# A 1 MB DRAM-to-DRAM copy on the weight queue, at the end of each step of a recurrent attention kernel

## The chip, the core and the metric

The kernel runs on one core of a Trainium2 chip; the other cores do nothing. The metric is the device time of one execution in microseconds (us), as a median over repeated executions.

## What is computed

The output mixes two branches row by row: `g * a + (1 - g) * b`, with `g = sigmoid(sum(x * gate_w))`. Branch `b` is a gated feed-forward block. Branch `a` is attention over segments of 32 rows with a memory of 8 rows, and the memory that one segment leaves is an input of the next, so the 64 segments have to be worked one after the other.

```python
def _A_ref(x, mem0, Wq, Wk, Wv, Wo, seg_len):     # x: 1 x 2048 x 1024, 32 heads of 128
    mem = mem0                                     # 8 rows
    for s in range(n_seg):                         # 64 segments of 32 rows
        h = jnp.concatenate([mem, x[:, 32*s:32*s+32]], axis=1)          # 40 rows
        q, k, v = (jnp.einsum('btd,dhe->bhte', h, W) for W in (Wq, Wk, Wv))
        p = _softmax(jnp.where(mask, q @ k.T * scale, -1e9))
        o = jnp.einsum('bhte,hed->btd', p @ v, Wo)
        mem = o[:, :M]                             # rows 0..7 feed the next segment
        outs.append(o[:, M:])

def _B_ref(x, w_gate, w_up, w_down):               # 1024 -> 3584 -> 1024
    return _gelu(x @ w_gate) * (x @ w_up) @ w_down
```

All inputs are bf16. Each of the four attention weights Wq, Wk, Wv, Wo is 1024 x 32 x 128 (or its transpose), 8.4 MB[...].

## The kernel before

The program first transposes x and works a small part of the feed-forward block while the attention weights are loaded. Then come the 64 steps of the recurrence (`for s in range(NSEG)`), one per segment, each about 23.5 us long. Then the rest of the feed-forward block runs (`for fb in range(NFB)`), which also mixes and stores the output.

**One step.** The weights are cut into 64 pieces of 128 x 2048 bf16 (512 KB): 8 pieces for each of K, Q, V, O and each half `r` of the heads. A step is a walk over these 64 pieces in a fixed order (`walk`). It starts with K and Q of the first half, one piece of each in turn (`both(0)`), then V of the first half, then K and Q of the second half (`both(1)`), then O of the first half mixed with V of the second, and last O of the second half. `proj(p, s)` issues the matmuls of piece number `p`: lines L820 and L803 for K, Q and V, L831 for O. Between the pieces, the dictionary `at`, filled by calls `on(m, r, n, f)`, holds the other work: `f` is called ahead of piece `n` of the block `(m, r)`. The tails are L870 (an output projection of rows that were put off, tile `oR`), L850 (projections made ahead for a later group, tile `hR`) and L1042 (the new memory rows go into the next step's `hT`).

**The weight stream.** Most pieces stay resident in slots (`sl`). The pieces named in `PAIRS` (3 of K, none of Q, 5 of V, 4 of O) share a slot between the two halves of the heads, and have to be loaded again in each step: 3 + 5 + 3 pieces of 512 KB, and half a piece, 256 KB, into the tile `oh` (the other half of that O piece stays resident). `proj` ends with `spent(k)`, which issues the next load into the slot just read. All of these loads are issued from SyncE (SP), in the order of the program, on one hardware queue (L394 for `sl`, L387 for `oh`); SP waits on a semaphore of TensorE until the slot is free and then issues.

Every DMA belongs to a *lane*, a semaphore of its own; a DMA on a lane waits for the lane's previous DMA to have landed.

**The end of a step on SP.** After the load of `oh` follow the small loads for later steps: `qkr` (L551, 128 KB, for the next step), `hT` (L543, 64 KB, for the step after next) and two of `vB` (L557, 32 KB each, for the next step). SP then waits for the first K piece of the next step to have been used, and issues the three K loads. The stores run on other queues: `o_scr<-oRc` and `a_scr<-a_bf` (64 KB each a step) on ScalarE's queue, a few small ones on GpSimd's.

The place that the change touches:

```python
            if not last:
                on("o", 1, 0, lambda: load_qk(s + 1))
                if s + 2 < NSEG:
                    on("o", 1, 0, lambda: load_h(s + 2))
                on("o", 1, 0, lambda: load_v(s + 1))
            if s % 4 == 2 and G + 1 < NG:
                on("o", 1, 4, lambda: load_r(G + 1))
```

Of the kernel before, what the change touches and what calls it, by code (L numbers as in the profile page):

```python
# [5 lines left out]
BF16 = mybir.dt.bfloat16  # L6
# [24 lines left out]
class _Prog:  # L31
# [47 lines left out]
    def op(self, eng, fn, rd=(), wr=(), lane=None, after=()):  # L79
        o = _Op(eng, fn)  # L80
        if lane is not None:
            ln = self.lanes.get(lane)
            if ln is None:
                ln = self.lanes[lane] = [self.new_sem(f"{self.name}_{lane}"), 0, None]
            if ln[2] is not None:
                o.deps.append(ln[2])
            ln[1] += 16
            o.sem, o.val, o.inc, o.need = ln[0], ln[1], 16, True
            ln[2] = o
        for r in rd:  # L90
            self._touch(o, r, False, lane is not None)
        for r in wr:
            self._touch(o, r, True, lane is not None)
        o.deps.extend(after)
        if eng == "pool" and lane is None:
            if self.pool is not None:
                o.deps.append(self.pool)
            self.pool = o
        for d in o.deps:
            d.need = True  # L100
        o.idx = len(self.ops)
        self.ops.append(o)
        return o
# [92 lines left out]
def bass_gated_mix__memory_aug_recurrent_mem_tr__geglu_ffn__prompt_kernel(  # L196
# [16 lines left out]
    S, D = xf.shape  # L213
    _, H, Dh = A_Wq.shape
# [17 lines left out]
    with ExitStack() as es:  # L232
# [19 lines left out]
        NJP = 4  # L252
        NJR = NJ - NJP
        g_scr = nc.dram_tensor("g_scr", [NFB, 128, NJP * FB], BF16)

        PB = [es.enter_context(nc.psum_tensor(f"pb{i}", [128, 512], FP32)) for i in range(8)]
        PBV = [p[:, :].bitcast(BF16) for p in PB]
# [97 lines left out]
        op = P.op  # L355
# [185 lines left out]
        def load_h(s, eng="sp"):  # L541
            t = hTs[s % 2]
            op(eng, lambda e: e.dma_start(t[:, :, :].rearrange("p k c -> p (k c)"), xq_scr[s // 4, :, s % 4, :]),  # L543
               rd=[("D", "xq", s // 4)], wr=[t.r()], lane=f"h{eng}{s % 2}")

        def load_r(G):
            op("pool", lambda e: e.dma_start(hR[:, :, :].rearrange("p k c -> p (k c)"), xr_scr[G]), rd=[("D", "xr", G)],
               wr=[hR.r()], lane="hr")

        def load_qk(s):  # L550
            op("sp", lambda e: e.dma_start(qkr[:, :, :, :].rearrange("p u m c -> p u (m c)"),  # L551
                                           qk_scr[s // 4, :, :, s % 4, :].rearrange("u p c -> p u c")),
               rd=[("D", "qk", s // 4, u) for u in range(2)], wr=[qkr.r()], lane="qkr")

        def load_v(s, us=(0, 1), eng="sp"):
            for u in us:
                op(eng, lambda e, u=u: e.dma_start(vB[:, u, :], v_scr[s][:, u].rearrange("i h c -> h i c")),  # L557
                   rd=[("D", "v", s // 4, u)], wr=[vB.r(128 * u, 128 * u + 128)], lane=f"vb{eng}{u}")
# [4 lines left out]
           wr=[gwb.r()], lane="gw")  # L563
# [359 lines left out]
        for s in range(NSEG):  # L923
# [12 lines left out]
            def on(m, r, n, *fs):  # L936
                at.setdefault(spot["k" if m == "q" else m, r][n], []).extend(fs)
# [78 lines left out]
            if not last:  # L1016
                on("o", 1, 0, lambda: load_qk(s + 1))
                if s + 2 < NSEG:
                    on("o", 1, 0, lambda: load_h(s + 2))
                on("o", 1, 0, lambda: load_v(s + 1))  # L1020
            if s % 4 == 2 and G + 1 < NG:
                on("o", 1, 4, lambda: load_r(G + 1))

# [189 lines left out]
```

## Time and profile before

| | before |
|---|---|
| median of 13 executions | 2164.41 us (2155.23 to 2174.27) |
| the profiled execution, its own time | 2168.27 us |
| its span in the profile | 2166.3 us |
| TensorE busy | 1991.2 us, 92% of the span |
| bytes moved by DMA | 512.79 MB, of it 467.16 MB on SP's queue |
| steps of the recurrence | about 130 to 1630 us of the span |

The span is the part that the profile covers; 2.0 us of the execution lie outside it. A busy share says how long an engine had work in flight. The chain of waits follows the work that ended last back to what released each piece. In the list of DMA issues, the last number is the median time from issue to landing. In a table of windows, "DMA share" is the mean busy share of the core's 16 DMA engines in that stretch (slightly over 1 where a packet's time reaches out of it), and GB/s what they moved.

### The profile page before, as it was taken

To read this page: it belongs to the slowest core of one execution; us is meant where nothing else is said; L and a number is where in the kernel's file an instruction comes from. 1 tells how busy PE (TensorE), PEld (TensorE's weight loads), DVE (VectorE), ACT (ScalarE), POOL (GpSimd) and SP (SyncE) were. 2 spreads that over 40 slices of the span, in tenths; PEclk is the share of its full clock that TensorE was granted. 3 is DMA by queue.
4 is the path that set the end of the run, shared out by engine and by line. 5 is a ranking of instruction groups with operands and counts; after the bars stand their busy time and mean duration, and the time that the engine had idled before them with its cause. 6 is when DMAs were issued, how large, how long until landed. Compare 5 with 4: busy or idle time off the path is not lost.

```text
span 2166.3 us, 77621 instructions
## 1 busy us (share of the span) xinstructions
PE 1991.2 (92%) x38220; PEld 958.8 (44%) x32556; DVE 938.2 (43%) x2056; ACT 650.5 (30%) x1330; POOL 291.1 (13%) x589
## 2 busy tenths in 40 slices
PE   7888999989999998989899898989888999999999
PEld 4334454454444445445444444444344334243343
DVE  6433443443444443444344344434434436263462
ACT  4323333333333332333233233323222213032130
POOL 7211111111111111111111111111110000000000
PEclk9999999999999999999999999999999999999999
DMA  9988888887888887888888788878889200001000
GB/s 363 358 304 266 307 303 279 289 302 271 296 303 274 305 309 257 283 284 300 263 305 306 263 282 294 298 254 297 288 287 372 94 21 30 31 30 30 25 25 20
DMA packets 259310, 512.79 MB, mean 237 GB/s; under 512 B 56080, under 2 KB 109200, under 8 KB 258984
## 3 DMA queue, kind: packets, MB, share of 16 engines
q1 hardware_dynamic: 216256, 467.16, 62.1%
q10 hardware_dynamic: 34136, 20.19, 3.3%
q0 software_dynamic: 8592, 20.49, 2.6%
q8 instruction: 278, 4.55, 0.9%
q14 instruction: 48, 0.39, 0.1%
HBM read 474.17 MB, written 33.55 MB: 234 GB/s over the span
## 4 chain that ended last, share of the span: by engine, by line
PE 74%; DMA 19%; issue 4%; ACT 2%; DVE 1%; SPq 0%; POOL 0%; ACTq 0%; POOLq 0%; DVEq 0%
PE pb L820 17%; PE pb L480 17%; PE pb L803 13%; DMA oh<-in_A_Wo_dram 9%; PE pb L831 8%; DMA sl<-in_A_Wv_dram 5%; PE pb L850 4%; PE pb L708 4%; PE pb L1168 4%; PE pb L870 2%; PE pb L1146 1%; PE pb L772 1%; DMA xr_scr<-xr 1%; ACT a_bf L694 1%; ACT vA L694 1%
## 5 line engine op out<-in xcount | busy, mean ns | idle before, releaser
L820 PE MATMUL pb<-sl,hT 128*32 128x512 bf16 x8192 | 712.7, 383 | 26.5 <-DMA sl<-in_A_Wv_dram 16.2
L820 PEld LDWEIGHTS pb<-sl,hT 128*32 128x32 bf16 x8192 | 235.5, 97 | 403.1 <-issue 276.7
L803 PE MATMUL pb<-sl,hT 128*32 128x512 bf16 x4096 | 405.6, 383 | 0.0
L831 PE MATMUL pb<-sl,oT 128*32 128x256 bf16 x7680 | 292.8, 276 | 62.4 <-issue 42.2
L831 PEld LDWEIGHTS pb<-sl,oT 128*32 128x32 bf16 x7680 | 205.4, 97 | 114.0 <-issue 71.3
L850 PE MATMUL pb<-sl,hR 128*32 128x512 bf16 x3072 | 228.9, 387 | 19.9 <-issue 8.8
L694 ACT ACTIVATE tok<-pb 128x512 bf16<-128x512 f32 x192 | 114.9, 598 | 299.9 <-PE pb L820 273.8
L480 PE MATMUL pb<-xT,wg 128*128 128x512 bf16 x768 | 183.1, 382 | 4.0 <-DMA wg<-in_B_w_gate_dram 4.0
L480 PE MATMUL pb<-xT,wu 128*128 128x512 bf16 x768 | 181.5, 379 | 0.0
L468 ACT ACTIVATE s<-pb 128x512 f32<-128x512 f32 x112 | 66.9, 597 | 290.5 <-PE pb L480 290.5
L1168 PE MATMUL pb<-wd,GT 128*32 128x512 bf16 x1568 | 152.4, 379 | 0.0
L803 PE MATMUL pb<-wd,GT 128*32 128x512 bf16 x1568 | 152.4, 379 | 0.0
L797 POOL COPY oRc<-oT 128x128 bf16<-128x128 bf16 x128 | 96.5, 754 | 390.1 <-DVE oT L697 390.1
L697 DVE CAST oT<-pb 128x256 bf16<-128x256 f32 x256 | 96.8, 420 | 120.0 <-PE pb L784 120.0
L469 DVE SCALAR_TENSOR_TENSOR tp<-s,pb 128x512 f32<-128x512 f32 x112 | 76.7, 685 | 126.6 <-ACT s L468 126.2
L694 ACT ACTIVATE vA<-pb 128x512 bf16<-128x512 f32 x128 | 76.4, 597 | 171.7 <-PE pb L820 171.7
L850 PEld LDWEIGHTS pb<-sl,hR 128*32 128x32 bf16 x3072 | 86.7, 98 | 91.6 <-issue 34.2
L697 DVE CAST hT<-pb 128x32 bf16<-128x32 f32 x63 | 12.1, 191 | 254.9 <-PE pb L1042 254.9
L480 PEld LDWEIGHTS pb<-xT,wg 128*128 128x128 bf16 x768 | 75.0, 98 | 97.0 <-issue 8.2
L743 DVE TENSOR_REDUCE st<-pb 128x8 f32<-128x320 f32 x128 | 62.9, 492 | 125.3 <-PE pb L737 125.2
L480 PEld LDWEIGHTS pb<-xT,wu 128*128 128x128 bf16 x768 | 75.2, 98 | 90.9 <-issue 0.5
L697 DVE CAST stg<-pb 128x512 bf16<-128x512 f32 x64 | 44.3, 692 | 159.6 <-PE pb L803 159.6
(111 smaller groups left out, 2179.6 us busy)
## 6 DMA issues: line engine op xcount, KB each, us to landing
sl<-in_A_Wv_dram SPq DMA_DIRECT2D x331, 512.0 KB, 8.5
sl<-in_A_Wk_dram SPq DMA_DIRECT2D x205, 512.0 KB, 6.0
sl<-in_A_Wo_dram SPq DMA_DIRECT2D x204, 512.0 KB, 6.7
oh<-in_A_Wo_dram SPq DMA_DIRECT2D x65, 256.0 KB, 7.5
sl<-in_A_Wq_dram SPq DMA_DIRECT2D x16, 512.0 KB, 12.9
qkr<-qk_scr SPq DMA_DIRECT2D x63, 128.0 KB, 7.3
qk_scr<-fqk ACTq DMA_DIRECT2D x29, 256.0 KB, 5.9
wd<-in_B_w_down_dram SPq DMA_DIRECT2D x7, 1024.0 KB, 15.0
```

Source lines behind the costliest of these rows:

```text
L468: op("act", lambda e: e.activation(s1[:, :], hg, ACTF.Square, scale=SQ), rd=[BK(bg)], wr=[s1.r()])
L469: op("dve", lambda e: e.scalar_tensor_tensor(out=t[:, :], in0=s1[:, :], scalar=1.0, in1=hg, op0=ALU.add, op1=ALU.mult), rd=[BK(bg), s1.r() ...
L480: ins = e.matmul(PB[bk][:, 0:FB], lhsT=w[:, kc, cc:cc + 128], rhs=x[:, :, :, kc, :].rearrange("p t i c -> p (t i) c"), start=(kc == 0), st ...
L694: op("act", lambda e: e.activation(o, i, ACTF.Copy), rd=rd, wr=wr)
L697: op("dve", lambda e: e.tensor_copy(o, i), rd=rd, wr=wr)
L708: ins = e.transpose(to, t[:, j * 128:(j + 1) * 128], ident[:, :])
L797: op("pool", lambda e: e.tensor_copy(oRc[:, u, :, :].rearrange("p c (g j) -> p g j c", g=4), diag), rd=[oT.r()], wr=[oRc.r(128 * u, 128 * ...
L803: return e.add_instruction(mybir.InstMatmult(name=nc.get_next_instruction_name(), start_tensor_calc=start, stop_tensor_calc=stop, tile_siz ...
L820: ins = again(e, g, *at, one, end) if k[0] == "q" else e.matmul(*at, start=one, stop=end)
L831: ins = e.matmul(PB[XO][32 * g:32 * g + 32, 0:256], lhsT=oT[:, gp_, 2 * jj + hh, 0:32], rhs=w[:, c:c + 256], start=(r == 0 and one and hh ...
L850: ins = e.matmul(PB[b][32 * g:32 * g + 32, :], lhsT=h[:, k[2], :], rhs=w[:, g * 512:(g + 1) * 512], start=(n == 0), stop=(n == 7))
L1168: ins = again(e, q, *a, j == 0, j == NJ - 1) if hf else e.matmul(*a, start=(j == 0), stop=(j == NJ - 1))
```

## The change

A DRAM tensor `warm` of 1 MB is declared, and in each step but the last a copy of the first 128 rows of Wk (128 x 4096 bf16, 1 MB, contiguous) into it is issued from SP, ahead of piece 4 of the block `("o", 1)`. Nothing reads `warm`. Its lane, `warm`, makes each copy wait for the copy of the step before.

```diff
         g_scr = nc.dram_tensor("g_scr", [NFB, 128, NJP * FB], BF16)
+
+        warm = nc.dram_tensor("warm", [128, H * Dh], BF16)
...
                 if s + 2 < NSEG:
                     on("o", 1, 0, lambda: load_h(s + 2))
                 on("o", 1, 0, lambda: load_v(s + 1))
+                on("o", 1, 4, lambda: op("sp", lambda e: e.dma_start(warm[:, :], A_Wk[0:128].rearrange("d h e -> d (h e)")),
+                                         wr=[("D", "warm", 0)], lane="warm"))
             if s % 4 == 2 and G + 1 < NG:
                 on("o", 1, 4, lambda: load_r(G + 1))
```

## Prediction, made before the changed kernel was run

> **What bounds the kernel now.** I read the page's slices first, then the chain of waits, then one step in the timeline of SP and in tables of windows.
>
> ```profile
> PE   7888999989999998989899898989888999999999
> DMA  9988888887888887888888788878889200001000
> PE 74%; DMA 19%; issue 4%; ACT 2%; DVE 1%; SPq 0%; POOL 0%; ACTq 0%; POOLq 0%; DVEq 0%
> ```
>
> TensorE is nearly full everywhere, the DMA engines are eight tenths full for as long as the recurrence lasts, and the chain passes through both. Neither number says what a megabyte more costs, so I look at one step (start, duration, line, what is issued):
>
> ```profile
> 1025.32 0.47 SPq L387 DMA_DIRECT2D oh<-in_A_Wo_dram  x1
> 1025.83 0.43 SPq L551 DMA_DIRECT2D qkr<-qk_scr  x1
> 1026.73 0.34 SPq L543 DMA_DIRECT2D hT<-xq_scr  x1
> 1027.83 1.16 SPq L557 DMA_DIRECT2D vB<-v_scr  x2
> 1033.97 1.30 SPq L394 DMA_DIRECT2D sl<-in_A_Wk_dram  x3
> 1037.43 2.33 SPq L394 DMA_DIRECT2D sl<-in_A_Wv_dram  x5
> ```
>
> and at the chain of waits in the same place:
>
> ```profile
> 1025.32 5.37 DMA oh<-in_A_Wo_dram
> 1030.69 0.04 issue
> 1030.73 0.40 PE pb L831 x7
> 1031.13 1.12 issue
> ```
>
> The loop of a step is: the first K slot is freed, the stream of 11 pieces and `oh` (5.77 MB) runs, `oh` lands last, TensorE finishes the step in about 3.2 us (1030.73 to 1033.97), and the next K slot is freed. The stream's end gates TensorE, so what delays the stream delays the step. Only the hole between two streams is free DMA time. Its size, in windows from 3.4 us ahead of the first K issue to 0.85 us behind it (last two columns: DMA share, GB/s), in three consecutive steps:
>
> ```profile
> 1006.88:1011.13 4.25, 3.15 (x80) 1.83 (x72) 0.19 (x1) 0.96 (x3) 0.29 (x1) 1.00 0.30 73
> 1030.57:1034.82 4.25, 2.93 (x72) 1.49 (x64) 0.62 (x2) 0.58 (x2) 0.34 (x1) 1.00 0.27 69
> 1053.53:1057.78 4.25, 3.81 (x96) 1.46 (x72) 0.88 (x2) 1.18 (x3) 0.42 (x2) 1.00 0.26 61
> ```
>
> The next three such steps have shares 0.22, 0.31 and 0.37. The mean is 0.29, so the hole holds 0.71 x 4.25 = 3.0 us of every engine's time.
>
> How the stream starts matters too. After the hole it is slow, while TensorE works `both(0)`; it is fast in the V block and slower again in `both(1)`, with no hole in front of that:
>
> ```profile
> 1034.82:1036.82 2.00, 2.00 (x44) 0.47 (x20) 0.00 (x0) 0.00 (x0) 1.99 (x4) 1.00 0.93 203
> 1037.40:1039.80 2.40, 2.40 (x64) 1.26 (x56) 0.92 (x2) 0.98 (x3) 0.00 (x0) 1.00 0.99 379
> 1039.80:1043.30 3.50, 3.50 (x72) 0.95 (x36) 2.71 (x8) 0.99 (x3) 0.22 (x1) 1.00 0.99 322
> 1043.30:1046.70 3.40, 3.38 (x124) 2.43 (x115) 1.93 (x5) 2.17 (x5) 1.25 (x3) 1.00 1.02 410
> ```
>
> The first 2.0 us give 192, 203, 242, 197, 195 and 206 GB/s in the six steps, mean 206.
>
> [...] SP's list of instructions for the changed kernel gives the copy as 16 x 32768, so all 16 engines work, 64 KB each; no copy of this kind is in the trace. [...] the queue named "instruction" moved 4.55 MB in 278 packets, 16.4 KB each.
>
> **The change, part by part.** It removes and moves nothing.
>
> *Issue on SP.* 63 more issues, at about 0.43 us (1.30 us for three K loads). SP is free from 1028.99, behind `vB`, until 1033.97, and the copy goes there. Its wait is for the copy of a step ago, about 23 us before. Nothing is queued behind it but the K loads, which wait for TensorE anyway. Cost nothing; the cover is 5.0 us.
>
> *The hole.* Issued at about -4.5 us before the first K load, and with some 0.9 us from issue to first data (1033.97 to the restart in the window at 1034.82), [...].
>
> *How long the copy holds an engine.* No DRAM-to-DRAM transfer is in the trace. Lower bound: the rate of the loads, 410 GB/s, makes 1.05 MB / 410 = 2.6 us. [...]
>
> *The stream.* [...] the K loads start 2.0 us late. They miss the slow 2.0 us: 206 x 2.0 = 412 KB, less the 64 KB of `a_scr` on another queue, so about 347 KB. If the slow start belongs to TensorE's `both` block, as the second slow stretch without a hole suggests, these bytes are made up at the end of the stream at about 390 GB/s, which is 0.9 us. If it belongs to the stream's own start, it moves along, and the full 2.0 us are lost. I take 0.9.
>
> *What of it reaches TensorE.* In some steps the queue runs dry before the O loads and swallows a delay. In the page `oh` needs 7.5 us to land in the median, against 5.37 in the step above, whose queue was short. So most steps have a backlog in front of `oh`. I choose 0.9 as the share that passes: 0.9 x 0.9 = 0.8 us a step. What is late next is `oh`, and the V pieces before it (L820 waits for them already).
>
> *Instruction blocks.* TensorE's "issue" idle ahead of L831 is its own starvation, around the end of a step:
>
> ```profile
> PE pb L831 <- issue: 45.7, 43, 2.2
> ```
>
> A fetch that falls beside the copy may wait behind a copy packet. Bounds: nothing, if packets are short or the block early; 1.1 us a step (45.7 / 43), if one more such stall arises in every step. I choose 0.3.
>
> *Other queues.* `o_scr` and `a_scr` stores share engines with the copy and land some us later. `a_bf` shares its place with the softmax tile `tA`, written some 9 us after that store's issue; cost nothing, unless the store takes that long.
>
> *Sum.* 63 x (0.8 + 0.3) = 69 us on the profiled execution's 2168.3 us, so 2237 us. That execution stands 3.9 us above the median of 2164.4, so I predict 2233 us.
>
> **The rivals.**
> 1. *The slow start moves with the stream* (22%). 2.0 x 0.9 + 0.3 = 2.1 us a step, 132 us, about 2297 us. For it: every stream starts at about 206. Against: the stretch at 1039.80.
> 2. *The copy fits the hole* (20%). [...] Only the instruction term is left, 0 to 19 us: 2164 to 2183 us. For it: the lower bounds. [...]
> 3. *Faster* (8%). The 206 GB/s is the price of a queue that had run empty, at the place of the first two K loads. A copy that bridges the hole saves up to (390 - 206) x 2.0 / 390 = 0.94 us a step. It decides below 3.0 + 0.94 = 3.9 us for the copy; at 3.0 us it makes 0.94 x 0.9 x 63 = 53 us, so 2111 us. Against: TensorE's block explains the slow stretches without it.
> 4. *Much slower* (10%). The copy takes 7 us or more, or instruction blocks stand behind 64 KB packets in each step: over 2310 us. [...]
>
> That the copy isn't made, or goes elsewhere, is excluded by SP's list: 63 more entries, each between `vB` and the first K load.
>
> **How the numbers follow.** My own case has 40%, 2195 to 2265 us. Against no change, a measurement of this kernel can tell about 0.3%, or 6.5 us. Rival 2 falls mostly within that or a little above: 12% for the same, 8% slower. Slower then is 40 + 22 + 8 + 10 = 80%, faster 8%. The range runs from 2157, the foot of rival 2, to 2310 us, and leaves out rivals 3 and 4.
>
> **What would show it.** In the profile after: 63 copies of 1024 KB on SP with a time to landing of about 6 to 7 us; 66 MB more written; a DMA share near 1 where it was 0.29; the first K piece landing about 2 us later against its issue; steps of about 24.6 us instead of 23.5; more time of the chain on `oh` and V. I am wrong if the copy lands within 4 us of issue, if the stream after it starts at over 350 GB/s, or if the steps grow while the K loads don't land later (then it is the instruction blocks).

## The result, and the profile after

| | before | after |
|---|---|---|
| median | 2165.88 us (48 executions) | 2201.58 us (11 executions, 2193.05 to 2214.12) |
| ratio to before, 95% interval | | 1.0167 (1.0146 to 1.0187) |
| span of the profiled execution | 2166.3 us | 2199.8 us |
| moved on SP's queue | 467.16 MB | 533.23 MB |

The kernel is slower by 1.7%, some 36 us or 0.57 us for each of the 63 copies. I had predicted 2233 us and a range of 2157 to 2310: the direction and the range hold, and the size is half of what I forecast.

The page of the changed kernel, slices and chain of waits, with the line on the DRAM:

```profile
PE   7888889998988898898999988999888999999999
DMA  9989999999999988999999999999999300000000
HBM read 540.23 MB, written 99.61 MB: 291 GB/s over the span
PE 67%; DMA 25%; issue 4%; ACT 2%; DVE 1%; POOL 0%; SPq 0%; ACTq 0%; POOLq 0%; DVEq 0%
```

The DMA digits went from 8 to 9 over most of the recurrence, the writes grew by 66.06 MB (63 copies of 1.05 MB), and DMA's share of the chain from 19 to 25%. TensorE's line of the page, before and then after:

```profile
PE 1991.2 (92%) x38220; PEld 958.8 (44%) x32556; DVE 938.2 (43%) x2056; ACT 650.5 (30%) x1330; POOL 291.1 (13%) x589
```

```profile
PE 2000.9 (91%) x38220; PEld 954.4 (43%) x32556; DVE 940.2 (43%) x2056; ACT 650.5 (30%) x1330; POOL 291.0 (13%) x589
```

The same 38220 matmuls kept it busy 9.7 us longer, so only 23.8 of the span's 33.5 us are idle time.

The copy sits where SP's list put it (timeline of SP, one step of the changed kernel):

```profile
1058.30 1.93 SPq L389 DMA_DIRECT2D oh<-in_A_Wo_dram  x1
1062.52 1.18 SPq L559 DMA_DIRECT2D vB<-v_scr  x2
1063.74 0.60 SPq L1023 DMA_DIRECT2D warm<-in_A_Wk_dram  x1
1068.25 2.47 SPq L396 DMA_DIRECT2D sl<-in_A_Wk_dram  x3
1071.70 2.61 SPq L396 DMA_DIRECT2D sl<-in_A_Wv_dram  x5
```

and it goes into the hole. These are windows from 3.4 us ahead of the first K issue to 0.85 us behind it in three steps of the changed kernel; the last two columns are DMA share and GB/s, as before:

```profile
1064.85:1069.10 4.25, 3.34 (x80) 1.64 (x72) 0.62 (x2) 0.58 (x2) 0.34 (x1) 1.00 1.01 320
1087.76:1092.01 4.25, 3.61 (x88) 1.27 (x64) 0.88 (x2) 1.18 (x3) 0.29 (x1) 1.00 0.94 299
1111.44:1115.69 4.25, 3.58 (x84) 1.23 (x64) 0.88 (x2) 1.18 (x3) 0.29 (x1) 1.00 0.92 291
```

The share there was 0.22 to 0.37; now it reads 0.92 to 1.01. That is too much: a table of windows counts a packet whole where it starts, and the copy's packets are long. With each packet's time counted only where it lies (worked out from the packets in the traces, from the third step to the last), the share of the hole goes from 0.26 to 0.83, and in the second profiles of the two kernels from 0.27 to 0.78.

The stream behind it starts worse. First three steps of before, then three of after, 5 us from 0.85 us behind the first K issue:

```profile
1011.13:1016.13 5.00, 5.00 (x112) 2.02 (x84) 1.12 (x2) 1.40 (x3) 0.00 (x0) 1.00 0.95 298
1034.82:1039.82 5.00, 5.00 (x112) 2.02 (x84) 1.12 (x2) 1.40 (x3) 2.35 (x5) 1.00 0.96 298
1057.78:1062.78 5.00, 5.00 (x88) 2.19 (x68) 1.54 (x3) 1.73 (x3) 0.00 (x0) 1.00 0.89 215
```

```profile
1069.10:1074.10 5.00, 5.00 (x112) 2.02 (x84) 1.12 (x2) 1.41 (x3) 2.35 (x5) 1.00 0.89 270
1092.01:1097.01 5.00, 5.00 (x88) 2.19 (x68) 1.54 (x3) 1.73 (x3) 0.00 (x0) 1.00 0.78 232
1115.69:1120.69 5.00, 5.00 (x88) 2.19 (x68) 1.54 (x3) 1.73 (x3) 0.00 (x0) 1.00 0.88 261
```

Single steps vary, but over six steps the means are 292 GB/s before and 252 after (over all from the third, 289 and 252). In 5 us that is 0.20 MB less, and at the 390 GB/s of the later stream 0.5 us a step. The lower share of these windows is not idle time: counted where it lies, the packets' share is 0.93 before and 0.94 after. The engines are still at work on the copy.

The packets show how far. The copy is 1008 packets of 65536 bytes, 16 for each copy. One takes 3.07 us in the median (2.4 to 4.7), and in 62 of the 63 copies all 16 are in flight together, for 1.4 us in the median. The copy is issued 4.0 us ahead of the first K issue in the mean; its first packet starts 2.4 us ahead of it, the last one 0.8 us ahead, and the last one ends 2.1 us behind it (2.3, 0.7 and 2.3 in the second profile). What spreads the starts over 1.6 us isn't shown: the trace doesn't name a packet's engine. By the shares above, 0.7 us of the hole stay empty on the average engine (0.9 in the second profile), and 0.5 us of the copy (0.6) lie behind the hole, where the K loads should run. The first K piece lands 5.8 us after its issue in the median (5.7 in the second profile) instead of 4.6.

The list of DMA issues (last number: median us to landing; K was 6.0 and `o_scr` 3.2 before):

```profile
sl<-in_A_Wk_dram SPq DMA_DIRECT2D x205, 512.0 KB, 7.0
warm<-in_A_Wk_dram SPq DMA_DIRECT2D x63, 6.5
o_scr<-oRc ACTq DMA_DIRECT2D x64, 64.0 KB, 6.2
```

Waits that are new (engine, what waited, for what: us in total, times, longest). The first line is of before, the other three of after:

```profile
PE pb L820 <- DMA sl<-in_A_Wk_dram: 0.7, 1, 0.7
```

```profile
PE pb L822 <- DMA sl<-in_A_Wk_dram: 8.0, 16, 1.0
PE pb L774 <- DVE tA L755: 6.3, 3, 2.8
DVE tA L755 <- DMA a_scr<-a_bf: 11.5, 4, 4.6
```

K pieces now come too late in 16 places at that line (1 and 3 in the two profiles of before), and in four steps the store of `a_bf` landed so late that the softmax tile sharing its place had to wait, and in three of them TensorE with it.

### The profile page after: what moved, and what is told of

It reads as the page before. It is cut to its first block, busy times and chain, and to the rows that moved or that the text cites. A ratio compares the mean times of both kernels' runs of the same rounds, so it can differ in the third digit from the quotient of the medians.

```text
span 2199.8 us, 77684 instructions
## 1 busy us (share of the span) xinstructions
PE 2000.9 (91%) x38220; PEld 954.4 (43%) x32556; DVE 940.2 (43%) x2056; ACT 650.5 (30%) x1330; POOL 291.0 (13%) x589
## 3 DMA queue, kind: packets, MB, share of 16 engines
q1 hardware_dynamic: 218272, 533.23, 69.5%
## 4 chain that ended last, share of the span: by engine, by line
PE 67%; DMA 25%; issue 4%; ACT 2%; DVE 1%; POOL 0%; SPq 0%; ACTq 0%; POOLq 0%; DVEq 0%
PE pb L482 16%; PE pb L822 14%; DMA oh<-in_A_Wo_dram 12%; PE pb L805 11%; PE pb L833 7%; DMA sl<-in_A_Wk_dram 5%; PE pb L1172 4%; PE pb L852 4%; PE pb L710 4%; DMA sl<-in_A_Wv_dram 3%; DMA a_scr<-a_bf 2%; PE pb L872 2%; PE pb L1150 1%; DMA xr_scr<-xr 1%; PE pb L774 1%
## 5 line engine op out<-in xcount | busy, mean ns | idle before, releaser
L822 PE MATMUL pb<-sl,hT 128*32 128x512 bf16 x8192 | 717.8, 384 | 49.8 <-issue 22.0
L822 PEld LDWEIGHTS pb<-sl,hT 128*32 128x32 bf16 x8192 | 231.6, 97 | 444.2 <-issue 284.5
```

The costliest lines, as they stand in the source:

```text
L822: ins = again(e, g, *at, one, end) if k[0] == "q" else e.matmul(*at, start=one, stop=end)
```

## The experiments

The theory after the result: **A**, the copy is hidden but for the engines that end it late; the K loads pay for that. Its rival: **B**, whatever meets the copy at the end of a step (instruction blocks, stores, DRAM traffic) pays. "Stalls" below are TensorE's idle times of over 0.4 us that the timeline puts to "issue", added up from the third step to the last. In every profile here such a stall ends 1.1 to 1.7 us after a 16 KB packet of the instruction queue has landed (one, of the 2 MB copy, after 0.8), where a tenth of all moments would do so by chance; I read them as waits for instruction blocks, as I call these packets.

**Size and place.** The copy cut to 512 KB:

```diff
-  e.dma_start(warm[:, :], A_Wk[0:128]...)
+  e.dma_start(warm[0:64, :], A_Wk[0:64]...)
```

> The copy is cut to 512 KB (64 rows), 32 KB on each engine. Theory A (the copy fills the hole, and only what reaches out of it into the K loads costs): a packet takes half of the 3.07 us, so about 1.5 us, ends well before the K loads come, and the kernel is within 5 us of before (ratio 0.999 to 1.003). Rival B (any copy there costs, by the stores it holds up, by its HBM writes or by instruction blocks): about half of the 36 us stay, 15 to 20 us (ratio 1.007 to 1.009).

Measured: 2194.33 us, ratio 1.0116 (1.0084 to 1.0149). Theory A falls as the whole story. The packets take 1.64 us and most of the K loads come on time (K waits of 3.5 us), yet some 25 us are lost. What grew is the stalls, 103 us against 76 in the first profile of before:

```profile
PE pb L833 <- issue: 53.4, 48, 2.2
PE pb L822 <- issue: 14.6, 14, 1.7
PE pb L852 <- issue: 12.8, 15, 2.2
```

Before, the first of these groups had 45.7 us, and the other two:

```profile
PE pb L820 <- issue: 8.0, 8, 1.8
PE pb L850 <- issue: 8.8, 13, 1.6
```

The copy doubled to 2 MB (`A_Wk[0:256]`, `warm` with 256 rows):

> The copy is 2 MB (256 rows), 128 KB on each engine, so about 6.1 us of each engine, and the K loads start about 3 us later than with 1 MB. If the slow first microseconds of the K loads belong to TensorE's K and Q block (which is over by then), the loads then start at over 330 GB/s, only the slow bytes are lost, and the step grows by 1.6 to 2.2 us against before: 100 to 140 us (ratio 1.046 to 1.065). If the slow start moves along with the stream, the loads start at about 200 GB/s again and the step grows by 3.0 to 3.6 us: 190 to 225 us (ratio 1.088 to 1.104).

Measured: 2379.79 us, ratio 1.0986 (1.0957 to 1.1015), at the upper expectation, but not for its reason alone. Waits of this kernel:

```profile
DVE tA L755 <- DMA a_scr<-a_bf: 175.2, 44, 7.2
PE pb L822 <- DMA sl<-in_A_Wk_dram: 76.7, 88, 2.6
PE pb L774 <- DVE tA L755: 55.9, 24, 3.3
```

The late store, which costs little with 1 MB, is now the longest new wait. From 4 to 6 us behind the first K issue, when TensorE is past its first K and Q block, three steps moved 188, 279 and 176 GB/s, and a fourth had hardly begun. That is under the 330 that my reason for the slow start asked for. The packets of all steps say the same: the K stream starts 3.9 us behind the first K issue here, and from 4 us on the DMA engines move 170, 211, 289, 353 and 387 GB/s in successive microseconds (means from the third step on). Before, it starts at 1.0 us, and from there they move 185, 243, 316, 351 and 387. The slow start moves along with the stream.

The 1 MB copy behind the K loads, in the middle of the stream:

```diff
-  on("o", 1, 4, lambda: op("sp", ... warm ...))
+  on("v", 0, 0, lambda: op("sp", ... warm ...))
```

> The same 1 MB copy, issued behind the three K loads, in the middle of the stream, where there is no hole. Theory A (the hole hides the copy): its 3.07 us of every engine now count in full, times the 0.9 that passes: 2.8 us a step, 175 us (ratio about 1.08). Rival C (the stream has slack, and the 36 us come from the end of the step, from the stores and instruction blocks there): less than 60 us (ratio under 1.03).

Measured: 2329.06 us, ratio 1.0756 (1.0729 to 1.0783), 165 us. Where there is no hole, the same bytes cost 2.6 us a copy instead of 0.57, and what waits is the V pieces:

```profile
PE pb L822 <- DMA sl<-in_A_Wv_dram: 125.7, 144, 2.4
```

The hole hides most of the copy. The exact share that passes isn't read from this, because TensorE's granted clock was lower as well, 0.957 in the profiled execution against 0.988 (last section).

**Packets.** The 1 MB copy in packets of 8 KB (`warm` declared with 64 more columns, written as `warm[:, 0:H * Dh]`):

> The same 1 MB copy at the same place, but the rows of the target are padded by 128 bytes, so that each engine gets 8 packets of 8 KB instead of one of 64 KB; the bytes are the same. Theory A (what counts is how long the copy holds the engines): the same time as the change, ratio about 1.017. Rival B ([...] holds up the o_scr and a_scr stores and the instruction blocks): the stores land as before, no wait of tA for a_scr is left, and half or more of the 36 us are gone (ratio 1.003 to 1.009).

Measured: 2198.54 us, ratio 1.0146 (1.0107 to 1.0186). The interval overlaps that of the change, so short packets save little or nothing here. tA's wait for a_scr fell to 0.9 us, from 11.5 and, in the second profile of the change, 7.1; K's stayed at 6.2 us, where the change has 8.0 and 9.0. That fits A for this size, and suggests that the late store of `a_bf` was a matter of the long packets, and a small one.

**Does a profile repeat?** The kernel before, once more:

> The kernel before, once more, for a second profile of it. If the idle time of TensorE behind instruction blocks (75.9 us in stalls over 0.4 us between the first and the last step in the first profile, none of it in the 6 us behind the first K load) says something of the kernel and not of one execution, the second profile has 70 to 82 us and again none in that stretch. If 20 us more or less is chance, it says nothing about the copies.

Measured: ratio 0.9986 (0.9968 to 1.0003). Stalls 66.8 us, a little under what I allowed, and again none within 6 us behind the first K load. So differences of 10 us between two profiles say nothing; I take those of over 20 us to say something.

The 512 KB copy, once more:

> The 512 KB copy once more, to see how far its time and its stalls repeat. If the stalls behind instruction blocks are its cost, the second profile has over 90 us of them again (before: 75.9 and 66.8 us), and the ratio is 1.008 to 1.015. If the 103 us were chance, it has 65 to 80 us.

Measured: 2193.63 us, ratio 1.0118 (1.0076 to 1.0160); stalls 93.3 us. Both repeat. The stalls are 27 us over those of before in the mean of two profiles, as much as the whole cost. How the copy brings them about is shown for a few only: 4 of 88 and 4 of 89 end with a block whose packet began as a packet of the copy ended.

The changed kernel, once more:

> The changed kernel once more, for a second profile. If its cost is the late K loads, the late a_scr store and the instruction blocks that meet the copy, all three are there again: TensorE waits for K pieces in 10 steps or more (none and one in the two profiles of before), tA waits for a_scr in some steps, and TensorE has 5 us or more of stalls behind instruction blocks in the 6 us behind the first K load, where before has none. If they were chance, one or more of them is gone while the time is the same.

Measured: 2200.75 us in its one execution. Waits for K at L822 9.0 us in 17 places, tA for a_scr 7.1 us in 5 steps. Stalls in the 6 us behind the first K load 9.3 us (11.5 in the first profile; none in either of before). In all it has 87.2 us of stalls, and the first profile 77.4. The K waits of before stood in 1 and 3 places at that line, not in none and one as I wrote; the contrast remains.

**A small one.** The copy cut to 128 KB (`warm[0:16, :]`, `A_Wk[0:16]`):

> The copy is cut to 128 KB (16 rows of Wk), 8 KB on each engine, some 0.3 to 0.4 us of it. If the 25 us of the 512 KB copy come from the engines being held when K loads, stores or instruction blocks want them, this copy costs at most a quarter of that: within 6 us of before (ratio 0.998 to 1.003). If a further DMA at that place costs whatever its size (an issue on SP, a semaphore, a wait), 20 us or more stay (ratio over 1.009).

Measured: 2169.57 us, ratio 1.0015 (0.9999 to 1.0032), stalls 68.4 us. A further DMA at that place costs little or nothing by itself: the interval ends at 7 us.

**Ahead of the small loads.** The 512 KB copy issued right behind `oh`:

```diff
+  on("o", 1, 0, lambda: op("sp", lambda e: e.dma_start(warm[0:64, :], A_Wk[0:64]...), ...))
   on("o", 1, 0, lambda: load_qk(s + 1))
```

> The 512 KB copy, but issued right behind oh and ahead of the small loads, so that it is over about 1 us sooner. If its cost is the K loads that start late on some engines, it is gone (ratio under 1.004). If its cost is instruction blocks and stores that meet the copy at the end of the step, or its HBM traffic beside oh, it stays: 15 to 30 us (ratio 1.007 to 1.014).

Measured: 2196.10 us, ratio 1.0157 (1.0121 to 1.0193); stalls 97.2 us, no wait for K worth naming. The K loads are not what the 512 KB copy costs.

The same place with the full 1 MB (*full_ahead* from here on):

> The 1 MB copy, issued right behind oh and ahead of the small loads. [...] the K loads are late by less or not at all. If the 36 us of the change are mostly the late K loads, 15 to 20 us are left (ratio 1.006 to 1.010) and the waits of TensorE for K and of tA for a_scr are gone. If they are mostly instruction blocks and what else meets the copy, 30 us or more stay (ratio over 1.014), as with the 512 KB copy put there.

Measured: 2253.81 us, ratio 1.0384 (1.0345 to 1.0424). It costs more than twice the change, and it separates the two theories best. TensorE's waits for K are down to 0.3 us and no wait for a_scr is left, but the stalls are some 142 us, about twice those of before:

```profile
PE pb L833 <- issue: 75.8, 48, 5.0
PE pb L822 <- issue: 20.9, 17, 1.9
PE pb L852 <- issue: 13.7, 9, 2.6
```

Of them 80 us lie within 5 us to 1 us ahead of the first K issue, where the two profiles of before had 46 and 34, and the longest single one is 5.0 us instead of 2.2. The copy lies 4 us sooner here (I had expected 1 of this place), and blocks come late beside it: of the 21 stalls of over 2 us in the last 5 us ahead of the K issue, 18 end with a block whose packet began within 0.02 us of the end of one of the copy's packets. With the blocks' times shifted by 0.3 to 0.7 us, 0 to 7 do.

The change itself delays blocks too. In before, 40 and 38 of them start between 1.5 us ahead of the first K issue and 0.5 us behind it, and 6 and 8 in the 2 us after that; with the change it is 11 and 5, and then 39 and 35. Few of these cost anything. TensorE takes 24 to 34 matmuls and weight loads a microsecond of its busy time in the first 5 us behind the K issue, and 58 to 61 in the stretch that full_ahead hits (5 to 2 us ahead of the K issue, in before), so there, as I read it, a late block is missed sooner. TensorE's granted clock was a little lower as well, 0.975 in the profiled execution against 0.988, which is part of the 3.8% (last section).

**Read, write, or packets?** A 512 KB store from a resident Wq slot instead of the copy:

```diff
-  e.dma_start(warm[0:64, :], A_Wk[0:64]...)
+  e.dma_start(warm[:, 0:2048], slots[home["q", 0, 0]][:, :])
```

> Instead of a DRAM-to-DRAM copy, a 512 KB store from a resident Wq slot to the same DRAM tensor at the same place, in packets of 4 KB: the DRAM write stays, the DRAM read and the long packets are gone. If the 512 KB copy costs by its long packets or by its DRAM reads, the store costs under 8 us (ratio under 1.004). If any 512 KB of DMA work or of DRAM writes at the end of the step costs, it is 20 to 30 us as with the copy (ratio 1.009 to 1.014).

Measured: 2179.58 us, ratio 1.0066 (1.0045 to 1.0087); stalls 90.7 us. Half of the copy's cost, between the two expectations: a store from on-chip memory, in short packets, is enough for part of it.

The 512 KB copy in packets of 4 KB (half of each of 128 rows of Wk, target rows padded):

> The 512 KB DRAM-to-DRAM copy as eight packets of 4 KB on each engine instead of one of 32 KB (half of each of 128 rows of Wk into a padded target); bytes, place and queue as with the 512 KB copy. If the long packets hold up the instruction blocks and stores, the cost falls from about 25 us to that of the 512 KB store, 8 to 16 us (ratio 1.004 to 1.008), and the stalls of TensorE behind instruction blocks fall from 103 us to under 90 us. If it is the engine time whatever the packets, it stays at 20 to 30 us (ratio 1.009 to 1.014).

Measured: 2194.39 us, ratio 1.0118 (1.0074 to 1.0161), like the 32 KB packets (1.0116 and 1.0118), though the stalls are 79.7 us and thus near before. It has waits for K of 5.9 us, and TensorE ran longer at half clock: 68 us of its execution, 45 to 53 us in the two with 32 KB packets. The time meets one expectation and the stalls the other. What is shown is that packets of 4 KB alone don't make this copy cheaper; why a store costs half of a copy stays open. Whether it matters that the copy reads rows of Wk, which the stream reads too, was not tried.

## Why the prediction was right, and off by half

- *Issue on SP, nothing.* Right. SP was free for it, and the 128 KB copy shows that the issue costs nothing measurable (ratio 1.0015, 0.9999 to 1.0032).
- *The hole of 3.0 us.* It is there: 3.1 us of the average engine are idle in it. But the copy takes the engines 2.2 us after its issue in the mean, 1.6 us on the first, not 0.9, and so leaves 0.7 to 0.9 us of the hole empty.
- *The copy's duration.* Wrong, and the term that was mis-sized. The K loads 2.0 us late stood for a copy that outlasts the hole of 3.0 us by as much; no trace of before has such a copy, and its duration was only my estimate. Measured: 3.07 us an engine on the average, close to the 2.6 us that the rate of the loads gave. Here 16 packets of 64 KB in 3.07 us are 342 GB/s each way while all of them are in flight; in full_ahead, further from the K loads, a packet takes 2.43 us, or 432 GB/s. Why it is slower in the change isn't shown.
- *Overrun 2.0 us, so 0.9 us of stream.* Measured 0.5 to 0.6 us on the average engine, 1.3 to 1.4 us on the last. It costs the stream 0.20 MB, 0.5 us. The stream itself is 6.03 MB with `oh`, not 5.77; no term rests on that.
- *What is late next: V and `oh`.* Not borne out. TensorE's waits for V pieces went from 20.3 and 23.8 us to 21.6 and 17.1, those for `oh` from 5.7 and 5.7 to 6.1 and 5.9. What came late was the K piece itself, which I had not counted.
- *Why the stream starts slowly.* The reason I preferred, TensorE's K and Q block, is not borne out: behind 2 MB, past that block, the loads ramp up as before. Nor is it mainly an emptied queue. The first 16 packets of K take 0.50 us in the mean before, 0.40 to 0.42 with the change and 0.24 behind 2 MB, but the 17th to 64th take 0.26, 0.29 to 0.31 and 0.26, and only the 129th to 256th are down to 0.17 to 0.18 in all three. So the slow start moves along with the stream, as rival 1 had it, though rival 1's cost needed the overrun of 2.0 us; and rival 3 (faster) falls. Why these packets are slow stays open.
- *Instruction blocks, 0.3 us.* That a fetch can wait behind the copy is borne out by full_ahead, where 18 of 21 long stalls end with a block that began as a packet of the copy ended. The size in the change is smaller and blurred: stalls of 77.4 and 87.2 us against 75.9 and 66.8, 11 us more in the mean or 0.17 us a step, which is no more than two profiles of one kernel differ by. Some 10 us in the stretch behind the first K load, where before has none, are there in both profiles.
- *Other queues, nothing, "unless the store takes that long".* In 4 and 5 steps it took that long: 6.3 and 2.8 us of TensorE.
- *The sum.* The waits that can be named are about 8 us more for K, 5 for tA and 11 in stalls, 24 of the 36 us. That is TensorE's added idle time: 23.8 us between the first profiles and 26.7 between the second. The other 12 us are mostly no wait at all. TensorE was busy 9.7 and 10.8 us longer for the same matmuls, of which some 3.5 us are half clock (an estimate: half of the 7 us more that it was busy in such stretches). What lengthened the rest isn't settled.
- *Rival 2*, the copy fits the hole, came close on the copy's duration, 2.6 us by the rate of the loads against 3.07. But the copy is not all in the hole: half a microsecond of it lies behind.

Direction and range were right because the costs that I named are real in kind. That the median also lies in the 2195 to 2265 us of my own case is in part luck: the copy was over-priced, while the late K pieces, the late store of `a_bf` and TensorE's longer busy time were not in the sum.

## What to carry over

A hole in the mean DMA share is not free for a transfer of that size: what counts is when the transfer really gets the engines (here 2.2 us after its issue), how far it reaches into the loads behind it (0.5 us on the average engine), and what else is fetched meanwhile. In these profiles small transfers on other queues and the instruction fetches showed up as a few long waits (4 of tA, up to 4.6 us) and as "issue" (stalls of 77.4 and 87.2 us in the change, some 142 in full_ahead). Before a transfer is put into a gap, look at how fast TensorE goes through its instructions there; 4 us of place changed the cost from 1.7 to 3.8%. And a table of windows that counts packets where they start misleads once a packet is as long as the window: here it showed a full hole (0.92 to 1.01 for 0.83) and idle engines behind it (0.78 to 0.89 for 0.94), and neither was so.

## What the runs showed of the hardware that I had not expected

TensorE's granted clock was lower in the kernels that made it wait long. The window over most of the recurrence (us, busy times, then granted clock, DMA share, GB/s), before and with the copy behind the K loads:

```profile
250.00:1600.00 1350.00, 1226.60 (x29312) 638.44 (x25668) 570.83 (x1441) 439.94 (x953) 197.36 (x441) 0.99 0.84 287
```

```profile
250.00:1600.00 1350.00, 1173.03 (x26728) 576.84 (x23413) 520.70 (x1311) 402.47 (x868) 180.18 (x402) 0.95 0.87 302
```

The second trace has 44 stretches at half clock (granted 0.5) against 11, some 4.6 us each, and TensorE's busy time grew from 1991.2 to 2059.4 us for the same work; with the 2 MB copy it is 39 stretches and 2062.5 us, with full_ahead 28 and 2016.7. The granted clock of these profiled executions was 0.957, 0.959 and 0.975, of before 0.988.

In such a stretch the matmuls come at half the rate. One such stretch of before lasts from 863.83 to 867.24 us:

```profile
866.16 0.84 PE L820 MATMUL pb<-sl,hT 128*32 128x512 bf16 x4
866.58 0.81 PE L803 MATMUL pb<-sl,hT 128*32 128x512 bf16 x4
867.01 0.60 PE L820 MATMUL pb<-sl,hT 128*32 128x512 bf16 x4
867.34 0.48 PE L803 MATMUL pb<-sl,hT 128*32 128x512 bf16 x4
867.56 0.48 PE L820 MATMUL pb<-sl,hT 128*32 128x512 bf16 x4
867.78 0.48 PE L803 MATMUL pb<-sl,hT 128*32 128x512 bf16 x4
```

Within it four matmuls start 0.42 us behind the four before them, after it 0.22 us. The stretches follow idle time: of the 4 us ahead of each of the eight in the recurrence of before, TensorE was busy for 0.46 to 0.57, against 0.91 in the mean of the recurrence, and only 2.5% of all moments there have so little. It need not be idle throughout. What sets the clock back is not shown beyond that.

So 68 of the 165 us, 71 of the 216 and 26 of the 87 of full_ahead are longer busy time and not waiting, most of it clock (an estimate: half of the busy time added at half clock is 66, 60 and 27 us). The change itself has 14 and 13 stretches, against 11 and 9.
